# Moving the q normalization and its crossbar transpose into the next tile's first GEMM

## The chip, the cores and the metric

The kernel runs on one core of one Trainium2 chip. Times are device microseconds of one execution. Each kernel was timed in rounds with the kernel before, on the same chip. A run counts as "slow" when it is over 1.5% above the fastest of its kernel; comparisons use the other runs, called fast. Ratios are the mean time of one kernel's fast runs over that of the other's fast runs of the same rounds, so they are not quite the ratio of the medians quoted beside them.

Engines: PE is TensorE (PEld its weight loads), DVE is VectorE, ACT is ScalarE, POOL is GpSimd, SPq is the sync queue, which here issues loads, stores and transposes in program order.

## The reference, cut to what matters

```python
def _attn_ref(q, k, v):                       # (8, 8, 576, 64) each
    q_s = np.exp(q - q.max(-1, keepdims=True))
    q_s = q_s / (q_s.sum(-1, keepdims=True) + 1e-09)
    k_s = ...                                 # softmax of k over the sequence
    kv = np.einsum('bhsd,bhse->bhde', k_s, v)
    return np.einsum('bhsd,bhde->bhse', q_s, kv)

def _moe_ref(x, w_in, w_out):                 # x: (4608, 512), d_ff 2048
    h = x @ w_in
    return np.maximum(0.01 * h, h) @ w_out
```

The attention output, reshaped to 4608 tokens, goes through the two GEMMs. There are 8 batches of 576 tokens and 9 GEMM tiles of 512 tokens.

## The kernel before: the parts that matter

The work is pipelined by tile `t`. Tile `t` runs GEMM1 (64 matmuls), then GEMM2 in four sub-tiles of 16 matmuls. In the slots between them it prepares attention: exponentials, casts and the q normalization of batch `t+2`, and the attention output ("po", which becomes the GEMM input `xT`) of batch `t+1`. A slot `(1, j)` lies in GEMM1 after the matmuls of block `j`; a slot `(2, s)` lies after sub-tile `s` of GEMM2.

```python
    def pair(name, dt=FP32):                 # two PSUM banks; the pool holds 4 pairs
        return ps_pool.tile([P, 2, 2048 // mybir.dt.size(dt)], dt, name=name, tag=BANKS)
    # ... cut ...
    def make_qnorm(st, b, gp, r0=0, r1=R):   # VectorE: reduce, reciprocal, multiply
            # ... cut ...
            nc.vector.reduce_sum(out=qsum[:, 0:n], in_=x, axis=AX.X)
            nc.vector.reciprocal(out=qrec[:, 0:n], in_=qsum[:, 0:n])
            nc.vector.tensor_tensor(out=x, in0=x, in1=..., op=ALU.mult)
    # ... cut ...
    def dma_transpose(st, b):                # the crossbar transpose of q, sync queue
        nc.sync.dma_start_transpose(out=qT_of(st)..., in_=qe_buf[b % 2]...)
    # ... cut ...
    def store(pout, t, t0, t1):              # the "store copy"; frees the pair pout
        out_sb = osb_pool.tile([P, 2, O], FP32, name="out_sb")
        nc.vector.tensor_copy(out=out_sb[:, k0:k1, :], in_=pout[:, k0:k1, :])
        # ... cut: four output DMAs from the sync queue ...
    # ... cut ...
    def slots_of(t):
        # ... cut ...
        n = t + 2
        if n < B:
            prep = prep_pieces(n, states[n])  # exp q0, norm q0, exp q1, norm q1, exp k0, exp k1, v cast
            put((1, NF - 1), prep[6:7])                                  # v cast
            put((2, 0), prep[4:6] + prep[0:4])                           # exps and norms
            put((2, NTS - 1), [lambda: dma_transpose(states[n], n)])     # after the last sub-tile
        if t + 1 < B:
            outs = out_pieces(t + 1)          # three po groups
            put((2, 2), outs[0:1])            # first group: copied out by ACT
            if n < B:
                put((2, 2), [kv_piece(states[n], n)])
            put((2, 2), outs[1:3])            # second and third group: copied out by DVE
        return slots
    # ... cut ...
    for t in range(NT):
        if t > 0 and t + 2 < B:
            load_batch(nc.sync, t + 2)        # q, k, v of batch t+2: 3.5 MB
        emit_moe(t, slots_of(t))
```

The softmax here doesn't subtract the row's maximum and nothing guards it: scores larger than these inputs give would overflow.

## Time and profile before

| | kernel before |
|---|---|
| median of the first 3 runs | 296.85 us (293.1 to 297.82) |
| span of the profiled run | 294.5 us |
| PE busy | 277.3 us, 94% |
| tiles 1 to 5 (prepare attention fully) | 33.71, 31.02, 30.41, 31.78, 33.48 us |
| tiles 6 and 7 (po alone, then nothing) | 28.35, 27.63 us |

The page's first lines: engine shares, then the granted PE clock in tenths over 40 equal slices.

```profile
PE 277.3 (94%) x2052; PEld 127.7 (43%) x2052; DVE 101.2 (34%) x129; ACT 119.0 (40%) x122; POOL 12.8 (4%) x23
...
PEclk9999999999799999999999999997999999999999
```

94% looks like a kernel with nothing left. The Trainium skill, "Trainium Kernel Development and Optimization", Performance Expectations, warns that matmul busy time is a bad metric for the distance to roofline, because matmuls are pipelined. The share misses a part. The two slices at 7 point to that part, because busy matmuls are slower in them: 16 matmuls take 5.31 us there and 3.63 us in the other tiles.

The tiles are better evidence. This is the windows view of the kernel before, one line per tile 1 to 5, then a stretch after the gap of tile 5, then tile 6. Columns: stretch, its length, busy time of PE, PEld, DVE, ACT and POOL with counts, granted PE clock (1.00 is full), DMA share, GB/s.

```profile
46.44:80.15 33.71, 31.99 (x298) 14.67 (x297) 21.11 (x26) 17.09 (x17) 0.00 (x0) 0.95 0.67 206
80.15:111.17 31.02, 29.35 (x218) 13.50 (x217) 11.93 (x14) 13.21 (x13) 0.00 (x0) 1.00 0.54 162
111.17:141.58 30.41, 29.34 (x218) 13.60 (x216) 11.47 (x13) 13.59 (x14) 0.00 (x0) 1.00 0.60 177
141.58:173.36 31.78, 29.35 (x218) 13.52 (x217) 11.74 (x13) 13.38 (x14) 0.00 (x0) 1.00 0.59 163
173.36:206.84 33.48, 31.03 (x217) 13.89 (x216) 12.00 (x13) 13.16 (x14) 0.00 (x0) 0.95 0.53 157
201.60:206.80 5.20, 5.20 (x20) 2.02 (x17) 2.27 (x3) 0.00 (x0) 0.00 (x0) 0.67 0.44 104
206.84:235.19 28.35, 28.35 (x145) 12.67 (x144) 4.80 (x4) 8.63 (x10) 0.00 (x0) 1.00 0.27 58
```

Tiles 1 to 5 differ from each other although they do nearly the same work, and tiles 1 and 5 have a granted clock of 0.95. The list of waits names what PE waits for. Columns: engine and tile that waited, what it waited for, total us, times, longest us.

```profile
DVE vb L172 <- DMA v_ld<-in_v_dram: 77.2, 5, 18.1
...
PE po L291 <- DVE out_sb L413: 7.8, 5, 2.3
...
PE po L291 <- ACT xT L307: 1.4, 4, 0.6
```

The first of these is the largest of the three, and not a loss by itself: VectorE is idle and waits. The second is PE's own. The timeline of tile 2 shows how the first leads to the second. Columns: start, length, engine, line, operation, count, and in brackets the idle time before it and what ended it. The timelines in this document are selections; lines between those shown are left out.

```profile
84.09 2.82 SPq L234 DMA_TRANSPOSE qT<-qe  x1
88.22 0.45 SPq L84 DMA_DIRECT2D v_ld<-in_v_dram  x1
93.96 10.52 PE L396 MATMUL pout<-w_out_sb,g_sb 128*128 128x512 bf16 x48
98.90 1.36 DVE L172 CAST vb<-v_ld 128x2304 bf16<-128x2304 f32 x1 [17.33 <-DMA v_ld<-in_v_dram]
100.18 1.34 DVE L185 TENSOR_REDUCE qsum<-qe 128x18 f32<-128x1152 bf16 x1
...
104.81 1.36 DVE L187 TENSOR_TENSOR qe<-qe,qrec 128x1152 bf16<-128x1152 bf16 x1
105.54 0.33 PE L291 MATMUL po<-qT,kd 64*64 64x320 bf16 x4 [0.18 <-ACT xT L307]
106.09 1.22 DVE L413 COPY out_sb<-pout 128x1024 f32<-128x1024 f32 x1
107.36 0.41 PE L291 MATMUL po<-qT,kd 64*64 64x256 bf16 x8 [1.49 <-DVE out_sb L413]
```

The first two sub-tiles of GEMM2 end at about 101 us (32 of the 48 matmuls that start at 93.96). Their pair could be copied out then. VectorE gets to it at 106.09, after a v cast that waited for its load and two normalizations of about 3 us each. PE then waits 1.49 us, because the third po group needs that pair.

### The profile page before, as it was taken

The numbers are of one execution on the slowest core, as the hardware profiler recorded it, in microseconds if no ns is written. First come the engines' busy times: TensorE is split into PE (matmuls) and PEld (weight loads), VectorE is DVE, ScalarE is ACT, GpSimd is POOL, SyncE is SP. The second block draws the span as 40 slices with busy tenths as digits, with TensorE's granted clock in tenths as the row PEclk, the third lists the DMA queues.
The fourth block names the chain that finished last, engine by engine and source line by source line (L and its number), as shares of the span: only waits on it lengthen the run. The fifth ranks groups of instructions, "written<-read, shape, count | busy, mean of one in ns | idle before, by whom it ended". The sixth has DMA issues, their size and how long they took to land.

```text
span 294.5 us, 4646 instructions
## 1 busy us (share of the span) xinstructions
PE 277.3 (94%) x2052; PEld 127.7 (43%) x2052; DVE 101.2 (34%) x129; ACT 119.0 (40%) x122; POOL 12.8 (4%) x23
## 2 busy tenths in 40 slices
PE   8799999999899979998999799996999999999994
PEld 3344444444344434444444344442444444444443
DVE  2830476819500581049101950076100410110012
ACT  5645445881055504571366215550451056006400
POOL 0831200000000000000000000000000000000000
PEclk9999999999799999999999999997999999999999
DMA  7999999990379316951597049903520330033014
GB/s 259 301 205 270 347 345 357 286 346 12 71 154 359 122 36 148 322 199 28 129 236 315 2 94 215 391 6 73 110 41 2 71 71 0 2 71 71 0 32 113
DMA packets 35908, 45.78 MB, mean 155 GB/s; under 512 B 15793, under 2 KB 20657, under 8 KB 35889
## 3 DMA queue, kind: packets, MB, share of 16 engines
q1 hardware_dynamic: 29328, 34.09, 40.2%
q0 software_dynamic: 6400, 11.27, 14.8%
q8 instruction: 16, 0.26, 0.4%
q10 hardware_dynamic: 160, 0.13, 0.2%
q14 instruction: 4, 0.02, 0.0%
HBM read 36.70 MB, written 9.44 MB: 157 GB/s over the span
## 4 chain that ended last, share of the span: by engine, by line
PE 47%; DMA 31%; DVE 13%; issue 3%; SPq 3%; ACT 2%; POOL 1%; DVEq 0%
PE ph L387 23%; PE pout L396 21%; DMA v_ld<-in_v_dram 18%; DMA w_out_sb<-in_moe_w_out_dram 7%; DVE qsum L185 4%; DMA w_in_sb<-in_moe_w_in_dram 3%; DVE qe L187 3%; DVE vb L172 2%; DMA k_ld<-in_k_dram 2%; DVE out_sb L413 2%; SPq L84 2%; ACT g_sb L442 1%; PE pout L425 1%; PE po L291 1%; DVE qrec L186 1%
## 5 line engine op out<-in xcount | busy, mean ns | idle before, releaser
L396 PE MATMUL pout<-w_out_sb,g_sb 128*128 128x512 bf16 x560 | 127.6, 386 | 0.6 <-DMA w_out_sb<-in_moe_w_out_dram 0.6
L387 PE MATMUL ph<-xT,w_in_sb 128*128 128x512 bf16 x576 | 126.0, 379 | 0.0
L442 ACT ACTIVATE g_sb<-ph 128x1024 bf16<-128x1024 f32 x72 | 73.6, 1024 | 105.1 <-PE ph L387 105.1
L387 PEld LDWEIGHTS <-w_in_sb 128*128 128x128 bf16 x576 | 56.3, 98 | 67.7 <-issue 0.2
L396 PEld LDWEIGHTS <-g_sb 128*128 128x128 bf16 x560 | 54.7, 99 | 68.4 <-issue 6.4
L413 DVE COPY out_sb<-pout 128x1024 f32<-128x1024 f32 (+1 forms) x18 | 21.4, 1193 | 80.1 <-PE pout L396 77.9
L172 DVE CAST vb<-v_ld 128x2304 bf16<-128x2304 f32 (+2 forms) x8 | 9.6, 1206 | 77.2 <-DMA v_ld<-in_v_dram 77.2
L185 DVE TENSOR_REDUCE qsum<-qe 128x18 f32<-128x1152 bf16 (+2 forms) x18 | 21.8, 1213 | 21.3 <-ACT qe L160 21.3
L187 DVE TENSOR_TENSOR qe<-qe,qrec 128x1152 bf16<-128x1152 bf16 (+2 forms) x18 | 22.0, 1225 | 0.6
L166 ACT ACTIVATE ke<-k_ld 128x1152 bf16<-128x1152 f32 x16 | 17.9, 1156 | 10.5 <-DMA k_ld<-in_k_dram 10.5
L160 ACT ACTIVATE qe<-q_ld 128x1152 bf16<-128x1152 f32 x16 | 17.9, 1151 | 4.0 <-DMA q_ld<-in_q_dram 4.0
L307 ACT CAST xT<-po 128x512 bf16<-128x512 f32 (+6 forms) x11 | 5.4, 529 | 34.7 <-PE po L291 34.7
L291 PE MATMUL po<-qT,kd 64*64 64x512 bf16 (+7 forms) x128 | 8.0, 296 | 9.8 <-DVE out_sb L413 7.8
L307 DVE CAST xT<-po 128x896 bf16<-128x896 f32 (+7 forms) x19 | 14.0, 781 | 3.6 <-PE po L291 3.6
L152 PE MATMUL scr<-wsrc 128*128 128x512 bf16 x36 | 9.7, 426 | 1.2 <-DVE wsrc L92 1.2
L291 PEld LDWEIGHTS <-kd 64*64 64x64 bf16 x128 | 3.2, 104 | 15.9 <-issue 14.4
L247 PE MATMUL pkv<-vb,ke 64*64 64x65 bf16 x576 | 6.7, 193 | 0.6 <-ACT vb L172 0.3
L247 PEld LDWEIGHTS <-ke 64*64 64x64 bf16 x576 | 6.2, 105 | 1.6 <-issue 1.2
L152 PEld LDWEIGHTS <-wsrc 128*128 128x128 bf16 x36 | 3.6, 107 | 6.1 <-issue 2.1
L186 DVE RECIPROCAL qrec<-qsum 128x18 f32<-128x18 f32 (+2 forms) x18 | 4.6, 254 | 0.6
L119 POOL DMA_DIRECT2D w_out_sb<-in_moe_w_out_dram x5 | 3.8, 767 | 3.7 <-DMA w_in_sb<-in_moe_w_in_dram 3.7
L116 POOL DMA_DIRECT2D w_in_sb<-in_moe_w_in_dram x5 | 3.9, 795 | 0.0
(28 smaller groups left out, 32.8 us busy)
## 6 DMA issues: line engine op xcount, KB each, us to landing
out_dram<-out_sb SPq DMA_DIRECT2D x70, 128.0 KB, 2.4
q_ld<-in_q_dram SPq DMA_DIRECT2D x5, 1152.0 KB, 6.1
k_ld<-in_k_dram SPq DMA_DIRECT2D x5, 1152.0 KB, 8.4
v_ld<-in_v_dram SPq DMA_DIRECT2D x5, 1152.0 KB, 10.7
q_ld<-in_q_dram POOLq DMA_DIRECT2D x2, 1152.0 KB, 18.4
k_ld<-in_k_dram POOLq DMA_DIRECT2D x2, 1152.0 KB, 20.2
v_ld<-in_v_dram POOLq DMA_DIRECT2D x2, 1152.0 KB, 20.2
w_in_sb<-in_moe_w_in_dram POOLq DMA_DIRECT2D x3, 512.0 KB, 10.0
```

The source lines that it names most:

```text
L152: nc.tensor.matmul(scratch["t"][:, 0, :], lhsT=wsrc[:, 0:P], rhs=wsrc, start=True, stop=True)
L160: nc.scalar.activation(out=qe_buf[b % 2][:, :, gs, :].rearrange("p r g d -> p g r d"), in_=st[nm][:, gs, :].rearrange("p g (r d) -> p g r ...
L166: nc.scalar.activation(out=ke_buf[b % 2][:, gs, :], in_=st[nm][:, gs, :], func=AF.Exp)
L172: (copy or nc.vector.tensor_copy)(out=v_buf[b % 2][:, g0:g1, :, 0:D], in_=st["v"][:, g0:g1, :].rearrange("p g (r d) -> p g r d", d=D),)
L185: nc.vector.reduce_sum(out=qsum[:, 0:n], in_=x, axis=AX.X)
L187: nc.vector.tensor_tensor(out=x, in0=x, in1=qrec[:, 0:n].unsqueeze(3).to_broadcast([P, n, 2, D]), op=ALU.mult,)
L291: nc.tensor.matmul(pos[par % len(pos)][hs, par, at : at + n], lhsT=kd_buf[b % 2][ps, gp, hp, :], rhs=states[b]["qT"][ps, c0 // D : c1 // D ...
L307: copies[0](out=dst, in_=pos[0][:, :, at : at + n])
L387: nc.tensor.matmul(ph[:, j % 2, :], lhsT=w_in_sb[:, cb, j * P : (j + 1) * P], rhs=x[:, cb, :], start=(cb == 0), stop=(cb == NB - 1),)
L396: nc.tensor.matmul(pout[:, tsub % 2, :], lhsT=g_sb[:, j, tsub * P : (tsub + 1) * P], rhs=w_out_sb[:, j, :], start=(j == 0), stop=(j == NF ...
L413: nc.vector.tensor_copy(out=out_sb[:, k0:k1, :], in_=pout[:, k0:k1, :])
L442: nc.scalar.activation(out=g_sb[:, 2 * jj : 2 * jj + 2, :], in_=ph, func=AF.Prelu, alpha=LEAKY_SLOPE)
```

## The change

The normalizations of batch `t+1` leave slot `(2, 0)` of the tile before and go to slot `(1, 1)` of tile `t`. The transpose goes to slot `(1, 2)`, so in the sync queue it now stands behind the tile's loads. The intent is to take the normalizations off VectorE where it is crowded, and the transpose out of the loads' way. No work is added or removed.

```diff
+        if 2 < t + 1 < B:
+            st1 = states[t + 1]
+            put((1, 1), [make_qnorm(st1, t + 1, 0), make_qnorm(st1, t + 1, 1)])
+            put((1, 2), [lambda: dma_transpose(st1, t + 1)])
         n = t + 2
         if n < B:
             prep = prep_pieces(n, states[n])
             put((1, NF - 1), prep[6:7])
-            put((2, 0), prep[4:6] + prep[0:4])
-            put((2, NTS - 1), [lambda: dma_transpose(states[n], n)])
+            put((2, 0), prep[4:6] + [prep[0], prep[2]])
```

## The prediction

> **What bounds the kernel now.** TensorE: the page shows PE busy 277.3 of 294.5 us (94%), the two GEMMs alone 127.6 + 126.0 us. From 46 us on, one 512-token tile follows another, and each should cost its matmuls alone: the last three tiles, which prepare nothing, take 28.4, 27.6 and 28.2 us (windows view). Tiles 2 to 5 take 30.9, 30.5, 31.8 and 33.5 us, so there are some microseconds each to win. They sit in one place, after the third sub-tile of GEMM2, where the attention output of the next tile ("po") is computed. The list of waits has "PE po, released by DVE out_sb": 7.8 us, 5 times, longest 2.31. By the timeline these are 1.43, 1.49, 0.50, 2.08 and 2.31 us in tiles 1 to 5. "PE po released by ACT xT" adds 1.4 us.
>
> **Why PE waits.** The third po group takes the PSUM pair of output sub-tiles 0 and 1, free only when VectorE has copied it to out_sb. In tile 2 those sub-tiles are done at about 101 us, but the copy runs at 106.09, because VectorE has two q normalizations in front of it (reduce 1.35, reciprocal 0.27, multiply 1.36 us each; about 6 us the two), which themselves queue behind the v cast, which waited for v_ld until 98.90.
>
> **A second cost.** Right after that gap the clock falls in two tiles: the 16 matmuls of sub-tile 3 take 5.31 us in tiles 1 and 5 instead of 3.63 in tiles 2 to 4 (granted clock 0.67 in 201.6 to 206.8). That is 1.7 us each, 3.4 us in all. The Trainium skill, "TensorE: Matmul & The Clock Gate", Part 1, says an idle activity window of about 3.4 us throttles the array and that the window runs free; here stretches of 3.3 us (tile 1) and 4.1 us (tile 5) of small matmuls and waits were followed by a drop, others of 3.3 and 4.0 were not.
>
> **What the change moves.** No work is added or removed. Five batches' normalizations leave the full VectorE queue of GEMM2 for the start of the next tile's GEMM1, where VectorE idles over 15 us ("vb, released by v_ld": 17.33 us in tile 2). The store copy should then run at about 101 us. The crossbar transpose (issue 2.8 us, landing 4.8 us) no longer stands before the loads in the sync queue, so loads go out about 3 us earlier (tile 2: 84 instead of 87.0) and v lands near 95.5.
>
> **The danger, costed.** The transpose now waits for loads. Tile 1 already has this order: issued at 57.13 it took 8.0 us of issue, 11.6 to landing, 3.7 us after v landed. In tile 2 the normalization ends near 87.6, the transpose lands near 99.5, and the first po needs it near 104.4: about 5 us to spare. I expect no wait.
>
> **On the critical path:** 7.8 us of gaps (all five) and 3.4 us of slow clock, since the low-activity stretch shrinks to about 2.3 us. The ACT waits (about 1.4 us) stay. 296.85 − 11.2 ≈ 285.6 us. Range 283.5 to 288.8. Faster by over 2%: 0.95; within 2%: 0.04; slower: 0.01.
>
> **What would show it.** "PE po, released by DVE out_sb" gone; sub-tile 3 at 3.63 us in all tiles; tiles 1 to 5 each near 30 us; v_ld landing 3 us earlier; transposes landing before the po matmuls; PE busy about 274 of 283 us.
>
> **What would make it wrong.** The transpose behind 3.5 MB of loads lands later than in tile 1, so po waits for qT; the normalization delays something in GEMM1; the third po finds another release just as late (kd, or ACT's copy); clock drops, which vary by run (293.1 to 297.82 before), persist.

## The result, and the profile after

| | before | after |
|---|---|---|
| median, same rounds (4 runs each) | 296.38 us | 283.12 us (282.81 to 283.62) |
| ratio of fast runs (297.82 us before is over the 1.5% and left out) | | 0.959, 95% interval 0.9508 to 0.9671 |
| span of the profiled run | 294.5 us | 281.6 us |
| PE busy | 277.3 us, 94% | 274.7 us, 98% |
| PE waits for the store copy | 7.8 us in 5 waits | none in the list |
| PE waits for ACT's xT copy | 1.4 us in 4 waits | 0.3 us in 1 wait |

The same lines of the page after:

```profile
PE 274.7 (98%) x2052; PEld 127.2 (45%) x2052; DVE 102.0 (36%) x129; ACT 118.7 (42%) x122; POOL 12.9 (5%) x23
...
PEclk9999999999999999999999999999999999999998
```

The windows view after, tiles 1 to 6, same columns:

```profile
46.50:76.73 30.23, 30.17 (x297) 14.20 (x296) 15.52 (x20) 17.09 (x17) 0.00 (x0) 1.00 0.72 227
76.73:105.93 29.20, 29.20 (x217) 13.49 (x216) 12.12 (x14) 13.10 (x13) 0.00 (x0) 1.00 0.58 179
105.93:135.52 29.59, 29.30 (x218) 13.66 (x217) 11.65 (x13) 13.48 (x14) 0.00 (x0) 1.00 0.58 176
135.52:164.86 29.34, 29.21 (x218) 13.50 (x216) 11.92 (x13) 13.27 (x14) 0.00 (x0) 1.00 0.61 178
164.86:193.96 29.10, 29.10 (x217) 13.52 (x216) 12.19 (x13) 13.06 (x14) 0.00 (x0) 1.00 0.65 179
193.96:222.31 28.35, 28.35 (x145) 12.63 (x144) 10.57 (x10) 8.63 (x10) 0.00 (x0) 1.00 0.27 58
```

All of the gain lies in tiles 1 to 5: they took 160.40 us together before and 147.46 after, 12.94 us less, and the spans differ by 12.9. Tile 6 is unchanged to the hundredth although VectorE now does 10.57 us of work in it instead of 4.80: the moved work is free there. The clock is 1.00 in every tile shown.

The list of waits after, for the same pairs (the middle one is no longer in it):

```profile
DVE vb L172 <- DMA v_ld<-in_v_dram: 39.6, 5, 8.9
...
PE po L291 <- ACT xT L307: 0.3, 1, 0.3
```

And the timeline of tile 2 after, where the tile begins at 76.73 us (80.15 before):

```profile
81.93 0.45 SPq L84 DMA_DIRECT2D v_ld<-in_v_dram  x1
...
84.22 7.89 SPq L234 DMA_TRANSPOSE qT<-qe  x1
90.55 10.52 PE L396 MATMUL pout<-w_out_sb,g_sb 128*128 128x512 bf16 x48
92.07 1.36 DVE L172 CAST vb<-v_ld 128x2304 bf16<-128x2304 f32 x1 [8.00 <-DMA v_ld<-in_v_dram]
97.65 1.23 DVE L413 COPY out_sb<-pout 128x1024 f32<-128x1024 f32 x1 [4.22 <-PE pout L396]
101.84 0.69 PE L291 MATMUL po<-qT,kd 64*64 64x320 bf16 x12
```

Counted from the start of the tile, v is cast at 15.3 us instead of 18.8, and the store copy starts at 20.9 instead of 25.9. It now waits for PE and no longer for VectorE's queue. The po groups follow without a wait.

### The profile page after: what moved, and what is told of

Read it like the earlier page. It is cut to its first block, busy times and chain, and to the rows that moved or that the text cites. A ratio compares the mean times of both kernels' runs of the same rounds, so it can differ in the third digit from the quotient of the medians.

```text
span 281.6 us, 4650 instructions
## 1 busy us (share of the span) xinstructions
PE 274.7 (98%) x2052; PEld 127.2 (45%) x2052; DVE 102.0 (36%) x129; ACT 118.7 (42%) x122; POOL 12.9 (5%) x23
## 4 chain that ended last, share of the span: by engine, by line
PE 91%; DMA 5%; ACT 1%; DVE 1%; POOL 0%; SPq 0%; issue 0%
PE ph L387 44%; PE pout L396 43%; DMA w_in_sb<-in_moe_w_in_dram 3%; DMA k_ld<-in_k_dram 2%; PE po L291 2%; PE pout L425 1%; ACT xT L307 1%; PE pkv L247 1%; SPq L84 0%; POOL w_in_sb L116 0%; PE pt L215 0%; DVE qT L225 0%; DVE vb L172 0%; DVE out_sb L433 0%; PE pt L373 0%
## 5 line engine op out<-in xcount | busy, mean ns | idle before, releaser
L396 PE MATMUL pout<-w_out_sb,g_sb 128*128 128x512 bf16 x560 | 124.2, 379 | 0.0
L396 PEld LDWEIGHTS <-g_sb 128*128 128x128 bf16 x560 | 53.9, 98 | 65.3 <-issue 1.3
L152 PE MATMUL scr<-wsrc 128*128 128x512 bf16 x36 | 11.0, 472 | 1.2 <-DVE wsrc L92 1.2
L258 DVE RECIPROCAL krec<-pkv 128x4 f32<-128x4 f32 (+1 forms) x9 | 1.6, 178 | 17.0 <-PE pkv L247 17.0
## 6 DMA issues: line engine op xcount, KB each, us to landing
v_ld<-in_v_dram POOLq DMA_DIRECT2D x2, 1152.0 KB, 19.7
```

The source lines that it names most:

```text
L152: nc.tensor.matmul(scratch["t"][:, 0, :], lhsT=wsrc[:, 0:P], rhs=wsrc, start=True, stop=True)
L396: nc.tensor.matmul(pout[:, tsub % 2, :], lhsT=g_sb[:, j, tsub * P : (tsub + 1) * P], rhs=w_out_sb[:, j, :], start=(j == 0), stop=(j == NF ...
```

## The experiments

Two halves of the change make the store copy earlier: the normalizations leave VectorE's queue, and the loads (hence the v cast in front) come earlier. My prediction put the first at the centre. The first four runs take the halves apart, bypass both, and test the clock alone.

### The transpose behind the loads, the normalizations left in place

```diff
         if 2 < t + 1 < B:
             st1 = states[t + 1]
-            put((1, 1), [make_qnorm(st1, t + 1, 0), make_qnorm(st1, t + 1, 1)])
             put((1, 2), [lambda: dma_transpose(st1, t + 1)])
 ...
-            put((2, 0), prep[4:6] + [prep[0], prep[2]])
+            put((2, 0), prep[4:6] + prep[0:4])
```

(edits to the changed kernel)

> Half of the change: the crossbar transpose goes behind the next tile's loads, the two normalizations stay where they were, in front of the store copy in VectorE's queue. Theory A (the store copy was late for two reasons that add up: the v cast waited for late loads AND the normalizations stood behind it): in tiles 2 to 5 v lands about 3.5 us earlier, the copy ends near the time PE needs the pair, gaps of 0 to 0.5 us are left; tile 1, whose loads do not move, keeps its 1.4 us gap and, in some runs, its slow clock. About 288 us, ratio near 0.972. Rival B, as my prediction put it (the normalizations' place is what matters): gaps of 1 us and more remain, 294 us or more.

Measured: 286.36 us median (285.19 to 287.18), ratio 0.9663 (0.9616 to 0.9710), faster than expected. In the timeline of tile 2 (it starts at 78.66) the normalizations stand in front of the store copy as before:

```profile
94.44 1.36 DVE L172 CAST vb<-v_ld 128x2304 bf16<-128x2304 f32 x1 [14.35 <-DMA v_ld<-in_v_dram]
...
102.80 1.22 DVE L413 COPY out_sb<-pout 128x1024 f32<-128x1024 f32 x1
...
104.08 0.55 PE L291 MATMUL po<-qT,kd 64*64 64x320 bf16 x12 [0.21 <-DVE out_sb L413]
```

The copy comes at 24.1 us of the tile, still 3.2 us later than in the changed kernel, yet only 0.21 us of wait is left. Tiles 2 to 5 take 29.36, 29.58, 29.34 and 29.39 us, in sum 0.44 us more than in the changed kernel. Tile 1 keeps its wait (1.61 us), as its loads do not move: it takes 32.20 us in this run. Two of the four runs (286.99 and 287.18 us) had a granted clock of 0.991, the other two (285.19 and 285.74 us, the profiled one) 1.000 and 0.998; so a slow clock most likely comes with it in some runs. The rival that only the place of the normalizations matters has fallen.

### The normalizations moved, the transpose still ahead of the loads

```diff
+            if t + 2 < B:
+                put((1, 3), [lambda: load_batch(nc.sync, t + 2)])
 ...
-        if t > 0 and t + 2 < B:
+        if t == 1:
             load_batch(nc.sync, t + 2)
```

(edits to the changed kernel)

> The other half: the normalizations move to the next tile's first GEMM as in the change, but the transpose still goes before that tile's loads, which are then issued about 10.4 us into the tile. Theory A: v lands about 22.3 us into the tile, its cast ends at 23.6, the store copy at 24.9, and PE needs the pair at 25.1: barely in time, 283.1 to 285.5 us, gaps of at most 0.8 us per tile. Rival C (it is the earlier loads that give the gain): gaps of over 1 us per tile, over 288 us.

Measured: 283.84 us median (283.49 to 284.0), ratio 0.9573 (0.9539 to 0.9607). Tile 2 starts at 76.28:

```profile
99.57 1.36 DVE L172 CAST vb<-v_ld 128x2304 bf16<-128x2304 f32 x1 [15.96 <-DMA v_ld<-in_v_dram]
...
100.85 1.21 DVE L413 COPY out_sb<-pout 128x1024 f32<-128x1024 f32 x1
...
102.11 0.55 PE L291 MATMUL po<-qT,kd 64*64 64x320 bf16 x12 [0.27 <-DVE out_sb L413]
```

The v cast is later than in the kernel before (23.3 us into the tile against 18.8), and still PE loses only 0.27 us here. So either half alone brings most of the gain: the store copy has a deadline, about 24 us into the tile, and each half alone brings it near that. The halves replace each other; they do not add. Only in tile 1, whose loads the change does not touch, is the normalizations' move needed.

### The kernel before with the store copy on the other engine

```diff
-        nc.vector.tensor_copy(out=out_sb[:, k0:k1, :], in_=pout[:, k0:k1, :])
+        copy = nc.scalar.copy if 1 <= t <= 5 and t0 == 0 else nc.vector.tensor_copy
+        copy(out=out_sb[:, k0:k1, :], in_=pout[:, k0:k1, :])
```

> The kernel before, with only the store copy of output sub-tiles 0 and 1 (tiles 1 to 5) moved from VectorE to ScalarE; normalizations, transposes and loads stay. Theory A (PE waits for this copy and nothing else of the old order): the waits of po for out_sb go, the slow clock goes, the short waits for ACT's xT copy (about 1.4 us in all) stay: 285.5 us, ratio 0.962. If something else of the old order cost time (the transpose ahead of the loads, VectorE's order itself), it stays above 289.

Measured: 283.14 us median (282.93 to 283.37), ratio 0.9551 (0.9517 to 0.9585), which is the time of the changed kernel. Normalizations, transposes and loads stand where they stood before: tile 2 starts at 76.31, v is cast at 95.24 (18.9 us into the tile, as before), and VectorE still normalizes q while the po groups run.

```profile
97.23 1.01 ACT L414 COPY out_sb<-pout 128x1024 f32<-128x1024 f32 x1 [0.46 <-PE pout L396]
...
101.15 1.36 DVE L187 TENSOR_TENSOR qe<-qe,qrec 128x1152 bf16<-128x1152 bf16 x1
101.33 0.78 PE L291 MATMUL po<-qT,kd 64*64 64x320 bf16 x12
```

Tiles 2 to 5 take 29.20, 29.58, 29.34 and 29.10 us, within 0.01 us of the changed kernel's. This settles the cause: nothing of the old order cost time that can be measured, except that it made this one copy late. It was even better than expected, because the waits for ACT's xT copy, expected to stay at 1.4 us, fell to 0.4 us; the PSUM runs below give the likely reason.

### The gap filled with matmuls

```diff
+    def fill_gap(n=5):
+        for _ in range(n):
+            nc.tensor.matmul(scratch["pout"][:, 1, :], lhsT=wsrc[:, 0:P], rhs=wsrc, start=True, stop=True)
 ...
-            put((2, 2), outs[1:3])
+            fill = [fill_gap] if 1 <= t <= 5 else []
+            put((2, 2), outs[1:2] + fill + outs[2:3])
```

(edits to the kernel before; the pair of the current sub-tiles 2 and 3 is handed over in `scratch["pout"]`, and its second bank is not yet in use)

> The kernel before, with five full-size matmuls of zeros (about 1.1 us) put into PE's wait in tiles 1 to 5, into a PSUM bank that is not yet in use. The gap stays as long, but PE is busy in it. Theory (the slow clock comes from the low activity around the gap): all 16-matmul blocks after the gap at 3.63 us, granted clock 1.00 in every tile; the gap of tile 3 (0.5 us) is overfilled by 0.6 us: about 294 us where the kernel before has two drops. Rival (the drop has nothing to do with activity): blocks of 5.31 us remain and the time is that of the kernel before, or 0.6 us more.

Measured: 293.73 us median (292.77 to 294.84), ratio 0.9909 (0.9877 to 0.9941). The gap is still there and the clock no longer falls. Tile 5 in the kernel before:

```profile
201.69 5.31 PE L396 MATMUL pout<-w_out_sb,g_sb 128*128 128x512 bf16 x16
```

And with the gap filled:

```profile
198.24 1.25 PE L158 MATMUL pout<-wsrc 128*128 128x512 bf16 x5
200.47 0.38 PE L297 MATMUL po<-qT,kd 64*64 64x448 bf16 x4 [0.97 <-DVE out_sb L419]
200.78 3.63 PE L402 MATMUL pout<-w_out_sb,g_sb 128*128 128x512 bf16 x16
```

All 6 runs had a mean granted clock of 0.998 to 1.000, and all 11 runs of the kernel before beside them 0.981 to 0.994. The rival, that the drop has nothing to do with activity, has fallen.

The timed runs of the kernel before give the price of a drop. Over the 33 runs beside these experiments, the fast ones (five are slow and left out) fall into three groups by mean granted clock: 0.992 to 0.994 at 294.2 to 294.9 us, 0.986 to 0.988 at 295.8 to 297.3, and 0.982 to 0.983 at 298.1 to 298.4. The profiled run, with two drops, had 0.988. So these are most likely one, two and three drops, at nearly 2 us each, and they are most of the spread of the kernel before. The changed kernel's runs lie within 0.8 us. What decides whether a gap is followed by a drop stays open. In the kernel before, the stretch from the first po group to the next sub-tile was 3.34 us long in tile 1 and 4.07 us in tile 5, with PE busy for 1.62 us of each, and both were followed by a drop; one of 4.04 us with 1.61 us busy (tile 4) was not.

### The PSUM pairs

The built programs differ in one place that the diff does not name. All PSUM pairs come from one pool, and the framework chooses which free pair an allocation gets. In the kernel before, the second po group took the pair of the first group (freed by ACT's copy) and the third that of output sub-tiles 0 and 1 (freed by the store copy). In the changed kernel it is the other way round, in tiles 1 to 5. I take it that the framework orders the pairs by when it expects them free; no run shows how it chooses. The waits of the other runs fit: where the copy came late (tile 1 of the first run above, with 0.29 us), the second group waits for ACT as in the kernel before. Where it came early (tiles 2 to 5 of that run, the run with only the normalizations moved and the run with the copy on ScalarE), the second group no longer does, and the gains of these runs most likely include the swap. Three runs write the pair of every allocation out by hand, which takes the choice away from it:

```diff
+    order = iter("...133 digits, one for each allocation...")
     def pair(name, dt=FP32):
-        return ps_pool.tile([P, 2, ...], dt, name=name, tag=BANKS)       # pool of 4
+        return ps_pool.tile([P, 2, ...], dt, name=name, tag=BANKS + next(order))   # 4 tags of 1
```

The control is the changed kernel with its own pairs:

> Control: the changed kernel, with the PSUM pair of each allocation written out by hand as the framework had chosen it for the changed kernel. Same program: 283.1 us within 0.3%.

The changed kernel with the old pairs:

> The changed kernel with the PSUM pairs that the framework had chosen for the kernel before (there the second po group takes the pair of the first po group, the third that of output sub-tiles 0 and 1; in the changed kernel it is the other way round). Theory D (the part of the gain that my prediction missed is the ACT wait, which this swap hides): the second po group waits for ACT's xT copy again, 1.1 us more in all over tiles 1 to 5, 284.2 us against the control's 283.1. Rival (the swap does nothing): the control's time, within 0.2 us.

The kernel before with the new pairs:

> The kernel before with the PSUM pairs of the changed kernel. Theory A: the swap alone gives no gain; the second po group now waits for the late store copy instead of the third, so the time is that of the kernel before to 1.5 us more. If the swap were the cause, it would be near 285.

Measured: 282.93 us median for the control (282.85 to 283.6), 283.72 with the old pairs (283.56 to 283.94), 298.29 for the kernel before with the new pairs (297.24 to 299.12; ratio to the kernel before 1.006, interval 0.9997 to 1.0123). The swap is worth 0.79 us by the medians of the first two, somewhat less than the 1.1 expected, and it is worth it only once the store copy is early. With the late copy it gains nothing: the waits for ACT are gone from the list, but the wait for the store copy, now at the second group, grows from 7.8 to 11.7 us.

```profile
PE po L298 <- DVE out_sb L420: 11.7, 5, 2.9
```

The two runs of the changed kernel also show where it goes: with the old pairs the second po group waits for ACT's copy 0.24, 0.56 and 0.27 us in tiles 1, 3 and 4; with the new pairs the third group meets it, 0.43 us in tile 3 alone. Tile 3 with the old pairs, then with the new:

```profile
131.58 0.47 PE L298 MATMUL po<-qT,kd 64*64 64x320 bf16 x8 [0.56 <-ACT xT L314]
...
131.26 0.33 PE L298 MATMUL po<-qT,kd 64*64 64x320 bf16 x4 [0.43 <-ACT xT L314]
```

### How much room the transpose has

In the changed kernel the transpose is issued 7.5 us into tile 2 and takes a median 11.1 us from issue to landing (4.8 before), so by this estimate it lands at 18.6; the first po group wants it at 24.3. Its issue also holds the sync queue for 7.89 us instead of 2.82. The Trainium skill, "DMA: Bandwidth & Descriptors", Queues, rings and completion order, says that on each DMA engine the descriptors of a ring are consumed in order, which fits: by this estimate the transpose lands about 3 us after v (cast from 15.3 us into the tile), not 4.8 us after its own issue. Two runs delay the normalizations, and with them the transpose, by added reductions on VectorE:

```diff
-            put((1, 1), [make_qnorm(st1, t + 1, 0), ...
+            put((1, 1), [stall(st1, t + 1, 4), make_qnorm(st1, t + 1, 0), ...     # 9 in the second run
```

> The changed kernel with four further reductions (1.35 us each, 5.4 us) on VectorE in front of the normalizations, so that the transpose is issued 5.4 us later, about 12.9 us into the tile. If there are over 5 us to spare for the transpose, as predicted, PE never waits for qT: 283 us within 0.5 us.

> The changed kernel with nine further reductions (12.1 us) in front of the normalizations. The transpose is then issued about 19.6 us into the tile, after the loads have landed, and lands some 4.7 us later at 24.3, just where the first po group wants it (24.27): 283 to 286 us, waits for qT of 0 to 0.6 us per tile. It tells how much room the transpose had.

Measured: 283.11 us (2 runs) with four reductions and 283.65 us (2 runs) with nine. With four, no wait for qT is in the list. With nine there is one, in tile 6:

```profile
PE po L299 <- DMA qT<-qe: 0.7, 1, 0.7
```

The delayed transposes land in 4.7 us (median of the second run), as the loads are through by then. So a delay of 12.1 us (nine reductions of 1.35) costs 0.66 us against the changed kernel on the same chip (282.99 us), as much as that one wait, and one of 5.4 us costs nothing that shows (282.93 us for the control on its chip). "about 5 us to spare" was on the careful side, and this danger was never near.

### The store copy delayed on purpose

```diff
-            put((2, 0), prep[4:6] + [prep[0], prep[2]])
+            put((2, 0), prep[4:6] + [prep[0], prep[2]] + [stall(states[n], n, 8)])
```

(an edit to the changed kernel: eight reductions between the v cast and the store copy)

> The changed kernel with eight reductions (10.8 us) put between the v cast and the store copy on VectorE in tiles 1 to 5. Theory A: the store copy is the gate, so the gap comes back one for one once the slack is used: about 3.2 us in each of tiles 2 to 5 and 6.9 us in tile 1, 19.7 us in all, plus slow clock after each (1.7 us a drop): 303 to 312 us. Rival (the copy's time does not matter): 283 us.

Measured: 315.26 us (314.9 and 315.61), ratio 1.0645, more than the 303 to 312 expected. The wait came back and its size was nearly right (19.7 us expected):

```profile
PE po L299 <- DVE out_sb L421: 20.9, 5, 6.0
```

The upper end of the expectation is 283.1 + 19.7 + 5 drops of 1.7 us = 311.3 us. Of the 4 us above it, the wait is 1.2. The waits for ACT's copy, which were left out, are 1.1: they are back at 1.4 us (0.3 in the changed kernel), at the second po group as in the kernel before. The clock is about 1.5: from the start of the third po group to the next tile it is 5.03 to 6.51 us here, against 3.73 to 3.81 in tiles 2 to 4 of the kernel before, some 10 us in all or 2 us a drop. All five tiles now drop after the gap: the windows of 4.1 to 5.6 us after it have granted clocks of 0.57 to 0.76, and the sub-tile takes 4.38 to 5.80 us for 15 recorded matmuls (one record is missing in each). Here the drop follows every wait of 3.4 us and more, while in the kernel before, with waits of 0.5 to 2.3 us, it followed one to three of five, if the granted clocks of the runs are read as above.

### A further step

ACT's copy of the first po group is the last thing in these tiles that PE waits for. One run issues that group one sub-tile earlier, beside the changed kernel once more as control:

```diff
-            put((2, 2), outs[0:1])
+            put((2, 1) if t >= 2 else (2, 2), outs[0:1])
```

> The changed kernel itself once more, as the control of the next run on the same chip: 283.1 us within 0.3%.

> The changed kernel with the first of the three po groups of each tile from tile 2 on moved one sub-tile earlier (after sub-tile 1 instead of 2), so that ACT's copy of it is long done when the third group wants its pair. What is left of the ACT waits in the changed kernel (0.29 us idle in tile 3, some 0.3 us hidden in the busy time of tile 4) should go: 0.3 to 0.9 us less than the control, 282.4 us. The transpose lands about 18.6 us into the tile and would now be needed at 20.9. Rival: a wait for qT shows up, or nothing changes.

Measured: control 282.99 us median (282.82 to 283.12), early group 282.77 (282.54 to 283.01), 6 runs each; 0.3 to 0.9 us less were expected. No wait for qT appeared, tile 3 fell from 29.58 us in the control to 29.16, but tile 6 grew from 28.35 to 28.58. The ranges overlap and 0.2 us is less than 0.1%: I do not call it faster.

## Why the prediction was right, and where its sizes were off

The direction and the mechanism held. The wait for the store copy was named from the list of waits, and all of it (7.81 us) went. The slow clock was named as a second cost, and it went: 1.68 us in each of two tiles. v was cast 3.4 us earlier in tile 2 (3 predicted). The transpose made nobody wait. PE was busy 274.7 of 281.6 us (274 of 283 predicted). The stretch of low activity in tiles 1 to 5 shrank to 1.4 to 1.9 us (2.3 predicted).

Point by point, what was off:

- **The sum.** The prediction took 11.2 us off 296.85; measured were 13.26 by the medians and 12.94 in tiles 1 to 5 of the profiles. 283.12 us lies 0.4 below the lower end of the stated range; by the ratio of the fast runs, 0.959 of 296.85 is 284.7 us, inside it. The mis-sized term is "The ACT waits (about 1.4 us) stay". They fell to 0.3 us, mostly because the rebuilt program swapped the PSUM pairs of the second and third po group: the run with the old pairs gives 0.79 us back, of the 1.09 by which these waits fell. I had read the order of operations from the diff and had not thought that the allocation could follow it.
- **The rest of the sum.** Of 12.94 us, 7.81 is the wait for the copy, 3.36 the clock (two drops) and 1.09 the ACT wait (1.38 less 0.29). The last 0.68 us is not in any listed wait; most of it (0.39) lies in tile 5. As the ends of matmuls are modelled in this profile, part of a short wait can be counted as busy time. The trace of the kernel before has a candidate in tile 5: ACT's copy of the first po group ends at 198.63 us and the second group starts at 198.68, with the same 0.05 us between them as at the listed wait for ACT in tile 2. It starts 0.92 us after the start of the matmuls before it (the product of k and v, 197.76), against 0.70 us in the changed kernel, so some 0.2 us may be an unlisted wait for ACT. No run shows that this is what it is; it stays open.
- **The place of the normalizations as the reason.** "VectorE has two q normalizations in front of it (...), which themselves queue behind the v cast" is true of the trace, but it reads as if the move were what counts. In tiles 2 to 5 the earlier loads alone did nearly as well (0.44 us short), and with the copy on ScalarE neither was needed (283.14 us). The reason is the deadline of one copy; the change moves it by two means of which one would have been enough there.

## What to carry to other kernels

When PE waits for a copy that frees a PSUM buffer, look at everything in front of that copy in its engine's queue, find its deadline, and ask which single thing must move; two movers may each suffice, and then their gains do not add. Here changing the engine of that one copy gave the whole gain of a larger rearrangement. After any reordering, compare the buffer addresses and waits of the two built programs too, because an allocator may change its choice, and add the slow clock that follows a gap to the gap's price.

## What the Trainium skill lacked or had wrong

- "TensorE: Matmul & The Clock Gate", Part 1, ties the throttle to an idle window of about 3.4 us; it also tells of a kernel whose clock swings because PE idles briefly and often, but gives no length of these idles. Here drops came after waits of 1.43 and 2.31 us, in stretches of 3.3 and 4.1 us in which PE also ran small (64x64) matmuls for 1.6 us, most likely in one to three of five such stretches by the run (granted clock of a whole run 0.994 to 0.982). Avoiding idle gaps of 3.4 us would not have been enough.
- The same page does not say what keeps the clock up in a gap that cannot be removed. Five full-size matmuls of zeros in the gap did: clock 0.998 to 1.000 in all 6 runs, 293.73 us against 296.25.
- "DMA: Bandwidth & Descriptors", DMA Transpose (X-bar), gives no time for a transpose that is queued behind loads. Here a 128x2304 bf16 transpose landed 4.8 us (median) after its issue ahead of the loads, and 11.1 us (median) behind 3.5 MB of them, and its issue held the sync queue for 2.8 and 7.9 us (tile 2).
- No page gives the time that loads lose to a transpose ahead of them in the sync queue: about 3 us here (v issued 8.1 us into tile 2 before, 5.2 after).
